# Attention's last turns in a fused attention, expert and dense kernel: choice of two groups behind the scores, first expert slot a turn earlier, v weighted three chunks ahead

## The chip, the cores and the metric

The kernel runs on one core of a Trainium2 chip. The metric is the device time of one execution in microseconds; lower is better.

## What is computed

A decayed linear attention over 4 x 768 tokens with 8 heads of 64, then a choice of one of 8 experts for each of the 3072 tokens with that expert's two-layer network, then a dense two-layer network. Cut from the reference:

```python
def _attn_ref(q, k, v):
    gamma = 1.0 - 2.0 ** (-5.0 - np.arange(H))
    for t in range(S):
        state = gamma * state + einsum('bhd,bhe->bhde', k[:, :, t], v[:, :, t])
        y[:, :, t] = scale * einsum('bhd,bhde->bhe', q[:, :, t], state)

def _moe_ref(x, modality_id, w_gate, modality_bias, w1, w2):
    logits = x @ w_gate + modality_bias[modality_id]
    e_idx = np.argmax(logits, axis=1)
    gate_w = softmax(logits)[arange(N), e_idx]
    for e in range(E):
        h = np.maximum(x[mask] @ w1[e], 0.0)
        out[mask] = gate_w[mask, None] * (h @ w2[e])

def _moe2_ref(x, w_in, w_out):
    h = x @ w_in
    return (h * sigmoid(1.702 * h)) @ w_out
```

## The kernel before

The work has three stages. **Attention** goes through NT = 24 chunks of 128 tokens in the loop `for n in range(LAST + 1)` (L861). One pass of this loop is called turn n here. The order of the instructions in the source is the order on each engine: the schedule is written by hand, and every engine (PE for matrix products, DVE and ACT for copies and element work, POOL for gathers and scatters, SP for loads) works through its own list in order.

In turn n a chunk passes through these helpers. `emit_prep` (L217) multiplies v by the decay on POOL and gives vs; before, it runs for chunk n + 2, with three buffers. `emit_scores` (L225) makes the scores pss of chunk n + 1 on PE (L231) and their masked copies A on DVE (L235, two of them). `emit_state` (L251) adds to the running state pst (L262) and copies it on ACT (ssb, L265). `emit_av` (L268) makes the chunk's output psy on PE (L279, L282), `emit_rows_k` (L238) turns the next keys (pkn L244, copy kn L246), `emit_xt` (L286) scales the output on DVE (xT, L290). One turn later `emit_rows` (L293) turns it into rows (pxr L297, copy xr L299) and writes them to memory (xd, from ACT's queue, L300), and `emit_gate` (L302) makes the gate's products (pm L305, copy lt on ACT L307). Two turns later `emit_logits` (L310) makes the logits (pl L311 on PE, lg L312 on DVE).

Tokens are sorted by expert in groups of GS = 3 chunks. `emit_group` (L314) is the choice: DVE works from the logits to ohall (L318 to L327), ACT makes ex (L321). `emit_rank` (L330) is the rank of each token within its expert: small products on PE (L334 to L339), then DVE arithmetic (L341 to L350) into posi and idg. `emit_scatter` (L352) writes them to the table `order` in memory by three indirect transfers from POOL (L354). Before, the choice of a group stands at the end of the turn that made its last logits, and its ranks in the next turn, after the state.

The **expert stage** works in slots of 256 tokens of one expert (`run_slots`, L633). `places` reads a slot's piece of `order` into ix (POOL, L641), `gather` fetches its rows xg (POOL, L650), `prep` turns them (pxt on PE L673, xh on ACT L676, xl on DVE L677). A slot has eight units: four of `b1` (first layer, 24 products L689 each, then hh on ACT L694 and hl on DVE L695) and four of `second` (second layer, 24 products pso, L707), in the order b1 0, b1 1, second 0, b1 2 and so on. Weights come as 512 KB loads raw from SP (L572, four buffers) and are split in two by `split` (L574): whi, a cast on ACT (L593), and wlo, a subtraction on DVE (L595). After each unit two more weights are split.

The first EARLY = 18 chunks' tokens suffice for two slots, whose table (`table_early`, L390) follows the ranks of chunks 15 to 17. Before, that is in turn 20; the slot's generator is then advanced by one step a turn (`next(slots)`), except in turn NT - 1 = 23. The first three steps only issue places and gathers; the fourth, in turn 24, turns the rows and does the first b1. EARLY_SPLIT splits one weight in turn 22 and two in turn 23, ahead of the slot. The loop ends with turn LAST = 26. The other slots follow after the final table (`table_final`, L410), which needs the last group's ranks.

The **dense stage** (`d1` L1094, `d2` L1114) runs from about 440 us to the end.

## Time and profile before

| | us |
|---|---|
| median of three runs | 999.86 |
| lowest and highest | 993.59, 1003.96 |
| profiled execution | 1001.46 |
| its span, first to last instruction | 999.8 |
| PE busy | 965.2 |
| DVE, ACT, POOL busy | 503.1, 410.7, 179.1 |

The span is what the trace shows; the profiled execution's time has 1.7 us around it. Times in the trace count from the span's start. In the timelines a bracket gives the idle time of the engine just before a row and what ended it. Attention takes about the first 134 us, the expert stage runs to about 440.

In the trace a turn can be told by its gate products (L305), which are those of chunk n - 1: turn 20 ends with them at 112.2, turn 21 at 118.4, turn 22 at 128.0, turn 23 at 132.3 and turn 24's at 134.3.

### The profile page before, as it was taken

Reading aid. Unit: us, or ns where it says so; the run is one execution under the profiler, and the core shown is the slowest. Engines: PE = TensorE matmul, PEld = TensorE weight load, DVE = VectorE, ACT = ScalarE, POOL = GpSimd, SP = SyncE. Lnnn points to the kernel's source line nnn. Section 1 sums busy time; section 2 is a strip of 40 time slices with the busy share of each in tenths; the row PEclk is TensorE's granted clock in tenths of the full one; section 3 lists DMA queues with packets and bytes.
Section 4 is the critical chain, followed back from the end, with each engine's and each line's share of the span. In section 5 each row is a group of like instructions: output and inputs, shape, how many; then the busy total and the mean of one; then the engine's idle time right before and its main releaser. Section 6 shows DMA issues by size and latency. Waiting matters only on the chain.

```text
span 999.8 us, 16732 instructions
## 1 busy us (share of the span) xinstructions
PE 965.2 (97%) x6610; PEld 855.2 (86%) x6610; DVE 503.1 (50%) x921; ACT 410.7 (41%) x728; POOL 179.1 (18%) x177
## 2 busy tenths in 40 slices
PE   8999879999999999999999999999999999999995
PEld 7888668899999987879999999998999998999994
DVE  3555568798888876449942322323323223223221
ACT  3433245576777665348732222222322223222221
POOL 2343334233322222003310010010100100100101
PEclk9999999999999999999999999999999999999998
DMA  8787689888888879925310100100001001000000
GB/s 288 225 217 199 126 217 227 265 271 285 284 266 270 282 242 333 324 67 177 127 43 1 33 32 1 33 32 22 27 17 32 32 1 33 32 1 1 32 1 31
DMA packets 43128, 128.18 MB, mean 128 GB/s; under 512 B 6976, under 2 KB 7360, under 8 KB 43040
## 3 DMA queue, kind: packets, MB, share of 16 engines
q1 hardware_dynamic: 34464, 107.96, 35.0%
q0 software_dynamic: 5120, 12.77, 3.7%
q10 hardware_dynamic: 3456, 6.29, 1.9%
q8 instruction: 53, 0.87, 0.4%
q14 instruction: 35, 0.29, 0.1%
HBM read 107.76 MB, written 19.24 MB: 127 GB/s over the span
## 4 chain that ended last, share of the span: by engine, by line
PE 54%; ACT 0%; DVE 0%; POOLq 0%; POOL 0%; issue 0%; ACTq 0%
PE psq L1121 27%; PE psd L1100 26%; PE pyt L1027 1%; ACT L1103 0%; POOLq L1187 0%; DVE ab L961 0%; DVE ab L963 0%; ACT o L1127 0%; ACT ab L956 0%; ACT ab L966 0%; ACT sig L1103 0%; DVE gl L1111 0%; DVE ab L962 0%; POOL out_dram L1129 0%; POOLq L1129 0%
## 5 line engine op out<-in xcount | busy, mean ns | idle before, releaser
L1105 DVE TENSOR_TENSOR g<-psd,sig 128x384 f32<-128x384 f32 x128 | 71.3, 557 | 279.7 <-ACT sig L1103 279.7
L1103 ACT ACTIVATE sig<-psd 128x384 f32<-128x384 f32 x128 | 62.9, 492 | 289.5 <-PE psd L1100 289.5
L1100 PE MATMUL psd<-yl,wih 128*128 128x384 f32 x512 | 172.1, 336 | 0.0
L1100 PE MATMUL psd<-yh,wil 128*128 128x384 f32 x512 | 171.9, 336 | 0.0
L1100 PE MATMUL psd<-yh,wih 128*128 128x384 f32 x512 | 171.6, 335 | 0.2 <-PEq L1076 0.2
L1121 PE MATMUL psq<-woh,gh 128*128 128x512 f32 x384 | 153.9, 401 | 0.7 <-ACT gh L1110 0.7
L1121 PE MATMUL psq<-woh,gl 128*128 128x512 f32 x384 | 152.2, 396 | 1.1 <-DVE gl L1111 1.1
L1121 PE MATMUL psq<-wol,gh 128*128 128x512 f32 x384 | 152.3, 397 | 0.0
L595 DVE TENSOR_TENSOR wlo<-raw,whi 128x1024 fp32r<-128x1024 f32 x93 | 113.4, 1224 | 32.6 <-ACT whi L593 29.3
L593 ACT CAST whi<-raw 128x1024 fp32r<-128x1024 f32 x96 | 99.9, 1046 | 42.0 <-issue 16.6
L689 PE MATMUL psh<-xh,whi 128*128 128x256 f32 x384 | 109.5, 285 | 0.2 <-ACT xh L676 0.2
L689 PE MATMUL psh<-xl,whi 128*128 128x256 f32 x384 | 107.9, 281 | 0.3 <-DVE xl L677 0.3
L689 PE MATMUL psh<-xh,wlo 128*128 128x256 f32 x384 | 107.7, 281 | 0.0
L1129 POOL DMA_INDIRECT out_dram<-o,idd x24 | 23.3, 973 | 462.5 <-DVE o L1125 387.5
L1111 DVE TENSOR_TENSOR gl<-g,gh 128x384 fp32r<-128x384 f32 x128 | 71.7, 560 | 65.0 <-ACT gh L1110 65.0
L1100 PEld LDWEIGHTS psd<-yh,wih 128*128 128x128 f32 x512 | 96.5, 188 | 6.3 <-PEq L1076 0.6
L1100 PEld LDWEIGHTS psd<-yl,wih 128*128 128x128 f32 x512 | 96.0, 188 | 5.8
L1100 PEld LDWEIGHTS psd<-yh,wil 128*128 128x128 f32 x512 | 96.1, 188 | 0.0
L1110 ACT CAST gh<-g 128x384 fp32r<-128x384 f32 x128 | 65.8, 514 | 70.3 <-DVE g L1105 70.2
L1121 PEld LDWEIGHTS psq<-woh,gl 128*128 128x128 f32 x384 | 72.1, 188 | 19.0 <-DVE gl L1111 1.5
L1121 PEld LDWEIGHTS psq<-woh,gh 128*128 128x128 f32 x384 | 72.0, 188 | 13.0 <-ACT gh L1110 1.0
L1121 PEld LDWEIGHTS psq<-wol,gh 128*128 128x128 f32 x384 | 72.3, 188 | 11.6
(195 smaller groups left out, 1516.4 us busy)
## 6 DMA issues: line engine op xcount, KB each, us to landing
raw<-in_w_dram SPq DMA_DIRECT2D x96, 512.0 KB
qk<-in_qn_dram SPq DMA_DIRECT2D x23, 512.0 KB
r<-in_w_in_dram SPq DMA_DIRECT2D x16, 512.0 KB
r<-in_w_out_dram SPq DMA_DIRECT2D x16, 512.0 KB
ys<-yo SPq DMA_DIRECT2D x12, 513.0 KB
yg<-ys SPq DMA_DIRECT2D x24, 256.5 KB
v<-in_kv_dram SPq DMA_DIRECT2D x24, 256.0 KB
xd<-xr ACTq DMA_DIRECT2D x24, 256.0 KB
```

The lines of the kernel that those rows point to most:

```text
L593: nc.scalar.copy(hi, raw)
L595: eng.tensor_tensor(out=lo, in0=raw, in1=hi.bitcast(F32), op=ALU.subtract)
L689: nc.tensor.matmul(ps[:, f, :], a[:, k, f * C:(f + 1) * C], b[:, k, :], start=(m == 0), stop=(m == 11), skip_group_check=True)
L1027: nc.tensor.transpose(ps[:, k, :], y[:, k * C:(k + 1) * C], ident)
L1100: nc.tensor.matmul(ps, a[:, k, f * C:(f + 1) * C], b[:, k, :], start=(m == 0), stop=(m == 11), skip_group_check=True)
L1103: nc.scalar.activation(sig, ps, AF.Sigmoid, scale=1.702)
L1105: V.tensor_tensor(out=g, in0=ps, in1=sig, op=ALU.mult)
L1110: nc.scalar.copy(gh, g)
L1111: V.tensor_tensor(out=gl, in0=g, in1=gh.bitcast(F32), op=ALU.subtract)
L1121: nc.tensor.matmul(PO[t][r], a[:, r * C:(r + 1) * C], b[f], start=(f == 0 and m == 0), stop=(f == NF - 1 and m == 2), skip_group_check=True)
L1129: nc.gpsimd.indirect_dma_start(out=outv[n], out_offset=bass.IndirectOffsetOnAxis(ap=idd[:, n:n + 1], axis=0), in_=o, in_offset=None)
```

## The change

Three things are moved.

- `emit_prep` runs for chunk n + 3 in turn n, with four buffers of vs, and three times ahead of the loop.
- For the two groups that end with chunks 17 and 20 (SOON), the turn in which their last logits are due makes the logits and the choice right behind the scores, ahead of the state, and the ranks and the scatter in the same turn. The first slot's table and generator therefore begin in turn 19, and the first b1 stands in turn 23. EARLY_SPLIT is set a turn earlier.
- At the end, the logits of chunk 23 follow its gate in turn 24, with the choice, and the last ranks come in turn 25, which is now the last. The scatter is issued ahead of the slot's step.

```diff
--- before.py
+++ after.py
@@ -218,7 +218,7 @@
         c = n % NC_
         d = st[n] = {}
         v = loads[n][3]
-        vs = wp.tile([C, H, D], F32, name="vs", tag="vs", bufs=3)
+        vs = wp.tile([C, H, D], F32, name="vs", tag="vs", bufs=4)
         nc.gpsimd.tensor_tensor(out=vs, in0=v, in1=b3(o1(M("kc")[:, 8 * c:8 * c + 8]), H, D), op=ALU.mult)
         d.update(vs=vs)
 
@@ -531,7 +531,7 @@
         return out_
 
     POOL = lambda i, kind: i in (9, 11, 13) or kind == 'S' and i % 2
-    EARLY_SPLIT = {NT - 2: 1, NT - 1: 2}
+    EARLY_SPLIT = {NT - 3: 1, NT - 2: 2}
 
     class Stream:
 
@@ -857,7 +857,9 @@
     load(3)
     grp = rank = slots = None
     mps = ExitStack()
-    LAST = NT + 2
+    emit_prep(2)
+    LAST = NT + 1
+    SOON = (EARLY - 1, EARLY + GS - 1)
     for n in range(LAST + 1):
         if n + AHEAD < NT:
             load(n + AHEAD)
@@ -866,18 +868,22 @@
         if n == 0:
             emit_state(0)
             emit_av(0)
-        if n + 2 < NT:
-            emit_prep(n + 2)
+        if n + 3 < NT:
+            emit_prep(n + 3)
         if n + 1 < NT:
             emit_scores(n + 1)
         if n + 1 < NC_:
             decay(n + 1)
-        if 0 < n < NT:
-            emit_state(n)
         m = n - 2
         pl = None
         if m >= 0:
             pl = ps_1.tile([C, 512], F32, name="pl", tag="pl")
+        soon = m in SOON
+        if soon:
+            emit_logits(m, grp, m % GS, pl)
+            emit_group(m - GS + 1, grp)
+        if 0 < n < NT:
+            emit_state(n)
         if n == 1:
             setup()
         scat = None
@@ -890,38 +896,44 @@
             emit_rows_k(n + 1)
         if n < NT:
             emit_xt(n)
+        if soon:
+            emit_rank(m - GS + 1, grp, pl)
+            scat = m - GS + 1
         if n == NT - 1:
             psl.close()
             open_psum(mps)
         if 0 <= n - 1 < NT:
             emit_rows(n - 1)
-        if 0 <= m < NT:
+        if 0 <= m < NT - 1 and not soon:
             if m % GS == 0:
                 grp = {"l": gp.tile([C, GS, E], F32, name="lg", tag="lg")}
             emit_logits(m, grp, m % GS, pl)
         if 0 <= n - 1 < NT:
             emit_gate(n - 1, ps_1.tile([C, C], F32, name="pm", tag="pm"))
+        if n == NT:
+            emit_logits(NT - 1, grp, GS - 1, pl)
+            m = NT - 1
+        if 0 <= m < NT and m % GS == GS - 1 and not soon and n <= NT:
+            emit_group(m - GS + 1, grp)
+            rank = (m - GS + 1, grp)
         if rank and n == LAST:
             emit_rank(*rank, pl)
             scat, rank = rank[0], None
-        if 0 <= m < NT and m % GS == GS - 1:
-            emit_group(m - GS + 1, grp)
-            rank = (m - GS + 1, grp)
-        if slots is not None:
-            if n != NT - 1:
-                next(slots)
-            if n < NT:
-                SS.split(EARLY_SPLIT.get(n, 0))
         if scat is not None:
             if scat + GS == EARLY:
                 for _ in table_early():
                     pass
             emit_scatter(scat)
-            if scat + GS == EARLY:
-                SS.limit, SS.ns = 8 * NP1, NP1
-                slots = run_slots(SS)
+        if slots is not None:
+            if n != NT - 2:
                 next(slots)
-                SS.load()
+            if n < NT:
+                SS.split(EARLY_SPLIT.get(n, 0))
+        if scat is not None and scat + GS == EARLY:
+            SS.limit, SS.ns = 8 * NP1, NP1
+            slots = run_slots(SS)
+            next(slots)
+            SS.load()
     psr.close()
     pa.close()
     open_more(mps)
```

The masks of the scores of chunk 23 (A) and the choice of chunks 18 to 20 on DVE, from xT of chunk 21 on, before:

```order
L290 TENSOR_TENSOR xT<-psy,qc 128x512
L312 TENSOR_TENSOR lg<-pl,brow 128x8
L235 TENSOR_TENSOR A<-pss,misc 128x512 x2
L290 TENSOR_TENSOR xT<-psy,qc 128x512
L312 TENSOR_TENSOR lg<-pl,brow 128x8
L318 TENSOR_REDUCE mx<-lg 128x3
L319 TENSOR_TENSOR lg<-lg,mx 128x24
L324 SCALAR_TENSOR_TENSOR cand<-lg,misc 128x24
L326 TENSOR_REDUCE best<-cand 128x3
L327 TENSOR_TENSOR ohall<-best,misc 128x24
L595 TENSOR_TENSOR wlo<-raw,whi 128x1024
```

and on the same engine at the same place after the change:

```order
L290 TENSOR_TENSOR xT<-psy,qc 128x512
L312 TENSOR_TENSOR lg<-pl,brow 128x8
L595 TENSOR_TENSOR wlo<-raw,whi 128x1024
L235 TENSOR_TENSOR A<-pss,misc 128x512 x2
L312 TENSOR_TENSOR lg<-pl,brow 128x8
L318 TENSOR_REDUCE mx<-lg 128x3
L319 TENSOR_TENSOR lg<-lg,mx 128x24
L324 SCALAR_TENSOR_TENSOR cand<-lg,misc 128x24
L326 TENSOR_REDUCE best<-cand 128x3
L327 TENSOR_TENSOR ohall<-best,misc 128x24
L290 TENSOR_TENSOR xT<-psy,qc 128x512
```

The first weight's subtraction wlo has moved ahead of the masks and the choice, and xT of chunk 22 behind it.

The rows of chunk 23 (xr, lt) and the first slot's casts on ACT, before:

```order
L299 COPY xr<-pxr 128x512
L300 DMA xd<-xr 128x512
L307 COPY lt<-pm 128x128
L676 CAST xh<-pxt 128x512 x2
L694 ACTIVATE hh<-psh 128x512
L593 CAST whi<-raw 128x1024 x2
L321 ACTIVATE ex<-lg 128x24
```

and on ACT after the change:

```order
L676 CAST xh<-pxt 128x512 x2
L694 ACTIVATE hh<-psh 128x512
L593 CAST whi<-raw 128x1024 x2
L299 COPY xr<-pxr 128x512
L300 DMA xd<-xr 128x512
L307 COPY lt<-pm 128x128
L321 ACTIVATE ex<-lg 128x24
```

The copies xr and lt have moved behind the first b1's hh and the two casts.

The end of the first b1 (L689) and the beginning of the second on PE, before:

```order
L689 MATMUL psh<-xh,wlo 128x256
L311 MATMUL pl<-misc,lt 128x8
L689 MATMUL psh<-xh,whi 128x256
L689 MATMUL psh<-xl,whi 128x256
L689 MATMUL psh<-xh,wlo 128x256
```

and on PE after the change:

```order
L689 MATMUL psh<-xh,wlo 128x256
L297 MATMUL pxr<-misc,xT 128x128 x4
L311 MATMUL pl<-misc,lt 128x8
L305 MATMUL pm<-xT,wgs 32x128 x4
L311 MATMUL pl<-misc,lt 128x8
L689 MATMUL psh<-xh,whi 128x256
```

The rows and the gate of chunk 23 and both last logits (the first L311 is chunk 22's, the second chunk 23's) now stand between the two units; before, chunk 23's rows and gate and chunk 22's logits stood ahead of the first.

## Rows read from the trace of the kernel before

**Rows 1.** The page's part 1: busy time of each engine, share of the span, instructions.
```profile
PE 965.2 (97%) x6610; PEld 855.2 (86%) x6610; DVE 503.1 (50%) x921; ACT 410.7 (41%) x728; POOL 179.1 (18%) x177
```

**Rows 2.** Windows: stretch, length, busy us by engine (instructions), PE clock, DMA share, GB/s.
```profile
115.00:120.00 5.00, 3.08 (x41) 2.43 (x40) 1.98 (x3) 0.37 (x1) 0.00 (x0) 1.00 1.26 51
120.00:125.00 5.00, 2.97 (x48) 2.64 (x48) 1.46 (x3) 1.71 (x4) 2.19 (x3) 0.82 0.63 185
125.00:130.00 5.00, 4.02 (x64) 3.22 (x58) 1.84 (x8) 1.91 (x4) 1.03 (x1) 0.84 0.74 290
145.00:150.00 5.00, 4.23 (x18) 3.40 (x18) 4.32 (x12) 2.69 (x4) 0.00 (x0) 0.70 0.88 200
200.00:240.00 40.00, 40.00 (x266) 36.62 (x265) 36.35 (x56) 28.39 (x39) 13.30 (x10) 1.00 0.81 277
```

**Rows 3.** PE's timeline: start, us, engine, line, operation, count, idle before and releaser.
```profile
107.09 1.16 PE L231 MATMUL pss<-qk 64*128 64x128 f32 x16
...
112.16 1.16 PE L231 MATMUL pss<-qk 64*128 64x128 f32 x16
...
122.03 1.16 PE L231 MATMUL pss<-qk 64*128 64x128 f32 x16 [3.63 <-ACT kn L246]
...
129.00 0.17 PE L334 MATMUL pl<-ohall,tri 128*128 128x24 bf16 x1 [0.98 <-DVE ohall L327]
...
133.17 0.63 PE L297 MATMUL pxr<-misc,xT 128*128 128x128 f32 x4 [0.86 <-DVE lg L312]
...
135.70 0.98 PE L673 MATMUL pxt<-misc,xg 128*128 128x128 f32 x7 [1.16 <-DMA xg<-xd,ix]
...
137.65 0.38 PE L689 MATMUL psh<-xl,whi 128*128 128x256 f32 x1 [0.34 <-DVE xl L677]
...
145.77 0.17 PE L334 MATMUL pl<-ohall,tri 128*128 128x24 bf16 x1 [2.12 <-DVE ohall L327]
```

**Rows 4.** ACT's timeline at the end of attention.
```profile
121.39 0.59 ACT L246 COPY kn<-pkn 128x512 f32<-128x512 f32 x1 [5.40 <-remote]
...
131.54 0.59 ACT L299 COPY xr<-pxr 128x512 f32<-128x512 f32 x1 [1.65 <-PE pxr L297]
...
132.53 0.27 ACT L307 COPY lt<-pm 128x128 f32<-128x128 f32 x1 [0.40 <-PE pm L305]
...
140.63 0.60 ACT L694 ACTIVATE hh<-psh 128x512 fp32r<-128x512 f32 x1 [3.28 <-PE psh L689]
141.13 1.99 ACT L593 CAST whi<-raw 128x1024 fp32r<-128x1024 f32 x2
```

**Rows 5.** DVE's timeline at the end of attention.
```profile
106.84 0.17 DVE L312 TENSOR_TENSOR lg<-pl,brow 128x8 f32<-128x8 f32 x1 [0.44 <-PE pl L311]
...
107.90 0.18 DVE L327 TENSOR_TENSOR ohall<-best,misc 128x24 bf16<-128x24 f32 x1
...
111.99 0.16 DVE L365 TENSOR_TENSOR t_cnt<-base,misc 128x8 f32<-128x8 f32 x1
...
123.22 1.29 DVE L235 TENSOR_TENSOR A<-pss,misc 128x512 f32<-128x512 f32 x2 [1.48 <-PE pss L231]
...
133.77 2.36 DVE L595 TENSOR_TENSOR wlo<-raw,whi 128x1024 fp32r<-128x1024 f32 x2 [0.68 <-ACT whi L593]
```

**Rows 6.** POOL's timeline at the end of attention.
```profile
108.22 1.04 POOL L222 TENSOR_TENSOR vs<-v,misc 128x512 f32<-128x512 f32 x1 [5.57 <-DMA v<-in_kv_dram]
111.14 1.00 POOL L354 DMA_INDIRECT order<-idg,posi  x1 [1.88 <-DVE idg L350]
...
122.20 0.59 POOL L641 DMA_DIRECT2D ix<-order  x1 [7.50 <-DVE lg L312]
...
128.82 1.03 POOL L650 DMA_INDIRECT xg<-xd,ix  x1 [4.41 <-DMA ix<-order]
```

**Rows 7.** SP's queue: the first four weight loads.
```profile
114.63 2.02 SPq L572 DMA_DIRECT2D raw<-in_w_dram  x4
```

**Rows 8.** PE's timeline where slot 2's rows are turned.
```profile
181.32 0.33 PE L673 MATMUL pxt<-misc,xg 128*128 128x128 f32 x1 [1.65 <-DMA xg<-xd,ix]
```

## The prediction

> **What bounds the kernel now.** I read the page's busy line first [rows 1]: TensorE (PE) is busy for 965.2 of 999.8 us, so an edit can only pay where PE idles or runs at a lower clock. The windows come next [rows 2]: the expert stage has PE full (40.00 of 40 us at clock 1.00 in 200:240), and the hole lies where attention ends, from 115 on: 115:120 has PE busy 3.08 of 5 us, 120:125 2.97 of 5 at a granted clock of 0.82, 125:130 0.84, and 145:150 0.70: TensorE spent parts of these at 1.2 instead of 2.4 GHz, after stretches in which it had idled. Last I read PE's own timeline there [rows 3], whose brackets name each wait. Adding them up: 3.63 (scores wait for the copy of kn), 0.98 (ranks wait for the choice), 0.86, 1.16 (transposes wait for gathered rows), 0.34, 2.12 (the last ranks wait for the last choice). Clock: (0.18 + 0.16) x 5 = 1.7 us lost in 120:130 and 0.30 x 5 = 1.5 us in 145:150.
>
> A turn of attention is 5.07 us of nearly unbroken PE work (107.09 to 112.16 [rows 3]). So starting the first slot a turn earlier moves no PE work away; it only changes which waits lie between the pieces. The forecast is a balance of waits.
>
> **What goes.** The ranks of chunks 18 to 20 and the last ranks now follow their choice in another way: the last choice is issued before the second b1 instead of behind it, so its 2.12 us go. The first b1 stands ahead of the last chunk's rows, so the waits in the old places (0.98, 0.86, 1.16, 0.34) go too, as far as new ones don't replace them. Together 5.46 us.
>
> **What comes at the early choice (turn 19).** The logits stand behind the scores; the choice is a DVE chain of 1.24 us (lg at 106.84 to the end of ohall at 108.08 [rows 5]) behind the two masks A (1.29). It ends some 2.6 us after the scores, while PE has about 3 us of state, values and row transposes to do before the ranks: no wait. The ranks' numbers are then ready near 108.1. The scatter doesn't start then: on POOL it is queued behind vs of chunk 22, which in the trace ran at 108.22 because v had only then arrived (5.57 us wait [rows 6]) and takes 1.05. So the scatter starts at about 109.3 instead of 111.14, 1.8 us sooner; vs three chunks ahead needs v a turn earlier and that costs POOL a wait, not PE. The table on DVE started at 111.99 [rows 5] and the weights' first load went at 114.63 [rows 7], 2.64 later; with the table at 108.1 the weights go at about 110.8, 3.8 us sooner.
>
> **The stall behind the first weight loads.** From 114.63 to 122.03 nearly everything halts: 115:120 moves 51 GB/s with the DMA engines busy 1.26 of the time, POOL waits 7.50 us for the scatter to land [rows 6], ACT's copy of kn starts at 121.39 after 5.40 us [rows 4], and PE idles. I can't name the cause; it begins where the first four 512 KB loads are issued, so I let it move with them, 7.4 us long. It then runs from 110.8 to 118.2. PE finishes turn 20 near 113.1 (turn 19 now carries logits and ranks, and 5.07 us follow) and idles 5.1 us. Before it was 3.63, and 0.3 more inside 115:120 (1.9 us idle there, of which 1.6 are the 3.63's beginning): 4.0. Cost +1.1; bounds +1.5 (PE a little earlier still) and -5.7 (no stall: the 4.0 us and the clock's 1.7).
>
> **New wait 1, ranks of turn 22.** Count from the end of turn 21's gate matmuls. ACT copies lt by +0.8, then casts whi (about 1.0) to +1.75. The first wlo now stands on DVE ahead of chunk 23's masks: 1.2 to +2.95, masks to +4.2, chain to +5.5. PE has 3.6 us of work before the ranks, so it waits 1.9 and ends the turn at +6.6. ACT's and DVE's durations are those of [rows 4, 5].
>
> **New wait 2, start of the first b1.** ACT: lt to +7.5, two casts to +9.4. DVE: two wlo (2.36) to +10.8, xT 0.69, lg, xl 0.7, to +12.3. PE's own work (values, rows, gate, 2.75, and the transposes 1.15) ends at +10.5: it waits 1.8 where 0.34 stood. The gathered rows: in the trace 24.6 us lie between the scatter's start (111.14) and the transposes (135.70). From 109.3 that gives 133.9; PE comes with stall and half-clock stretch at 118.2 + 4.9 + 1.7 + 9.35 = 134.2, so the gather is just hidden; bound +1.5 if it is later.
>
> **New wait 3, the last logits.** Behind the first b1 PE does rows, logits of 22 and the gate of 23 (1.1 us), then the logits of 23, in order ahead of the second b1. These need lt of 23, and ACT has hh (0.6) and two casts (1.99 at 141.13 [rows 4]) queued ahead of xr and lt; xr to the end of lt is 1.3 us (131.54 to 132.80 [rows 4]). That is 3.9 us after the b1's end, and DVE reads the logits of 22 only behind hl and two wlo, about the same. PE waits 3.9 + 0.2 - 1.1 = 3.0 us. In the old order lt was copied ahead of xh, and no wait stood there. Bounds 2.0 (casts overlapping more) and 3.3.
>
> **Sum.** 1.9 + 1.8 + 3.0 - 5.46 = +1.2; with the stall +1.1, +2.3 us. The clock: one low stretch behind the stall, one behind the 3.0 us wait, in place of two: 0 (bounds -1.5, +1.7). The profiled execution took 1001.46 us and would become 1003.8. It lies 1.6 above the median of 999.86, inside the spread of the runs (993.59 to 1003.96); against the median the forecast is 1002.2. Behind the second b1 the orders are alike, and PE is full, so a shift there reaches the end.
>
> **A rule weighed.** POOL waited 7.50 us for the scatter to land and the gather 4.41 more for ix, 128.82 being 14.2 us after the first weight load [rows 6, 7]. The Trainium skill, "DMA: Bandwidth & Descriptors", section on queues, rings and completion order, says that a transfer's semaphore write lands only after every earlier write of that DMA engine, in whatever queue. The two waits agree with it; no run here shows it alone. By that rule small transfers end no sooner than the weights begun before them, and the weights now begin before two of the three scatters.
>
> **Rivals.**
> 1. The forecast, chance 0.5: 1002.2.
> 2. The stall is not tied to the weights and doesn't come, chance 0.2. For: the loads of the expert stage show none (277 GB/s in 200:240 [rows 2]). Against: it begins within about a microsecond of the first loads. Sum +1.2 - 5.7 = -4.5: 995.4. As a mechanism of this kernel, if ix still came 14.2 us after the first weight load (125.0) and the rows 6.9 us later (128.82 to 135.70), at 131.9, PE would reach the transposes at 113.1 + 4.9 + 9.35 = 127.3 and the first b1 would start at 134.3 instead of 130.3, 4.0 late: 999.4. By the rule above this second number holds.
> 3. The change does what it says: DVE and ACT get ahead of PE because it is the one held up, new waits 1 and 2 vanish (-3.7), and the second low stretch of the clock with them (-1.5): 997.0. Chance 0.15. Against: ACT's and DVE's queues are in order and the casts are ahead.
> 4. Slower: the gather of slot 2. In the trace PE waited 1.65 us for it at 181.32 [rows 8]. The last scatter waits for the ranks' numbers, which DVE now computes behind hl and two wlo, with PE not waiting there any more. If that chain is not paced by PE, the wait grows by the 2.12 us that PE no longer loses at the last ranks, and a third low stretch of the clock adds 1.7: 1006.0. It decides once the last scatter starts later behind the last ranks than hl, two wlo (2.36) and the 1.3 us of rank arithmetic explain. Chance 0.15.
>
> **How the numbers follow.** A measurement of this kernel tells about 1% (10 us) from no change; the runs of before alone spread that far. All four cases lie within it. Faster by over 1% needs case 2 and 3 at once: 0.07. Slower by over 1% needs 4 and a longer stall: 0.05. The range runs from rival 2 less the clock's 1.5 (993.9) to rival 4 plus 1.
>
> **What would show it.** Right: scatter of the first groups near 109.3, weights issued near 111, a PE stop of about 5 us right behind turn 20; a wait of 1 to 2 us at the ranks of turn 22; a wait of about 3 us at the second L311 behind the first b1, ended by ACT lt or DVE lg; no wait at the last ranks. Wrong: no stop after the first loads, or the last logits passing without a wait.

## The result, and the profile after the change

The changed kernel is slower: a median of 1009.58 us (1005.84 to 1013.30, six runs) against 998.27 us (993.59 to 1003.96, six runs) for the kernel before, ratio 1.0106 with a 95% interval of 1.0076 to 1.0137. The forecast was 1002.2 us with a range up to 1007.0: wrong by 7.4 us, and outside its range. The profiled execution took 1005.84 us, the fastest of the six, so its span of 1004.2 (before 999.8) shows 4.4 us of a loss whose median is 11.3. More than that was lost behind turn 19, though: its gate products start at 102.90 here and at 106.73 in before, 3.8 us sooner with no less work done. That lead isn't the change's doing as far as the traces tell, since the same code has them anywhere up to 112.56 (last section); from turn 19 to the end this execution lost 4.4 + 3.8 = 8.2 us.

The page's busy line, as [rows 1]: PE's work is the same, 0.2 us apart.

```profile
PE 965.4 (96%) x6610; PEld 856.9 (85%) x6610; DVE 507.3 (51%) x921; ACT 410.6 (41%) x728; POOL 177.6 (18%) x177
```

The windows of the same stretches, as [rows 2], and 160:200 besides (stretch, length, busy us by engine with instructions, granted clock of PE, DMA share, GB/s):

```profile
115.00:120.00 5.00, 3.52 (x66) 2.99 (x65) 3.04 (x7) 1.58 (x5) 0.00 (x0) 1.00 1.21 268
120.00:125.00 5.00, 4.23 (x51) 3.13 (x51) 4.73 (x13) 3.02 (x6) 2.19 (x3) 0.66 0.75 279
125.00:130.00 5.00, 1.05 (x14) 0.76 (x14) 1.54 (x3) 0.85 (x2) 3.56 (x4) 0.84 0.72 225
130.00:135.00 5.00, 2.42 (x9) 1.83 (x9) 0.38 (x1) 0.73 (x2) 1.58 (x2) 0.50 0.38 144
135.00:140.00 5.00, 4.85 (x28) 4.64 (x28) 1.00 (x2) 0.60 (x2) 1.95 (x2) 0.64 0.54 105
...
145.00:150.00 5.00, 5.00 (x32) 4.69 (x31) 1.24 (x4) 1.58 (x3) 0.00 (x0) 0.66 0.54 204
160.00:200.00 40.00, 34.45 (x210) 30.64 (x209) 31.15 (x81) 16.37 (x21) 13.35 (x11) 0.96 0.72 213
```

The hole has moved and grown: 125:135 has PE busy 3.47 of 10 us (before 7.60), and the granted clock is below 1 in six of the seven stretches shown. Adding (1 - clock) x 5 over 120 to 150 gives 8.5 us where [rows 2] and the rest of before's windows give 3.2; part of that lies in time in which PE idles anyway.

PE's own timeline, as [rows 3] and [rows 8], with each wait in its bracket:

```profile
120.46 0.17 PE L334 MATMUL pl<-ohall,tri 128*128 128x24 bf16 x1 [1.94 <-DVE ohall L327]
...
131.52 0.48 PE L673 MATMUL pxt<-misc,xg 128*128 128x128 f32 x1 [5.47 <-DMA xg<-xd,ix]
133.06 1.76 PE L673 MATMUL pxt<-misc,xg 128*128 128x128 f32 x7 [1.06 <-DMA xg<-xd,ix]
...
143.99 0.36 PE L311 MATMUL pl<-misc,lt 128*128 128x8 f32 x2 [3.27 <-DVE lg L312]
...
148.41 0.24 PE L334 MATMUL pl<-ohall,tri 128*128 128x24 bf16 x1
...
167.50 0.50 PE L707 MATMUL pso<-whi,hl 128*128 128x512 f32 x1 [3.30 <-DVE hl L695]
...
186.54 0.69 PE L673 MATMUL pxt<-misc,xg 128*128 128x128 f32 x2 [2.00 <-DMA xg<-xd,ix]
```

Read them in order. The ranks of turn 22 wait 1.94 us: forecast 1.9. The transposes of the first slot wait 5.47 + 1.06 us for the gathered rows: forecast "just hidden". The last logits wait 3.27 us: forecast 3.0. The last ranks have no bracket: forecast none. Then a wait that the forecast doesn't have, 3.30 us for hl in the middle of a second layer; before it was 0.27.

These waits come to 15.04 us (1.94, 5.47, 1.06, 3.27, 3.30) where before has 9.36 (the six of [rows 3] and 0.27). Of the 8.2 us some 2.5 are left (an estimate) for the lower clock and the smaller gaps.

The 3.27 us are two queues that end together, as the forecast had them. ACT has hh, two casts, xr and lt in a row; lt ends at 143.75. DVE has hl, two wlo and then lg of chunk 22, which ends at 143.84 and is what PE's bracket names; PE starts 0.15 us behind it.

```profile
139.84 0.60 ACT L694 ACTIVATE hh<-psh 128x512 fp32r<-128x512 f32 x1 [4.40 <-PE psh L689]
140.33 1.98 ACT L593 CAST whi<-raw 128x1024 fp32r<-128x1024 f32 x2
142.21 0.59 ACT L299 COPY xr<-pxr 128x512 f32<-128x512 f32 x1
...
143.48 0.27 ACT L307 COPY lt<-pm 128x128 f32<-128x128 f32 x1 [0.68 <-ACT xr L299]
```

```profile
141.40 2.36 DVE L595 TENSOR_TENSOR wlo<-raw,whi 128x1024 fp32r<-128x1024 f32 x2 [0.24 <-ACT whi L593]
143.68 0.16 DVE L312 TENSOR_TENSOR lg<-pl,brow 128x8 f32<-128x8 f32 x1
```

POOL and SP, as [rows 6] and [rows 7]. The three scatters begin 7 us sooner than before, the weights 8.3 us sooner, and these now go out before the third scatter. POOL then waits 13.54 us for the scatters (before 7.50), with vs of chunk 23 queued behind:

```profile
104.16 1.00 POOL L354 DMA_INDIRECT order<-idg,posi  x1 [4.40 <-DVE sm L348]
105.47 0.97 POOL L354 DMA_INDIRECT order<-idg,posi  x1 [0.30 <-issue]
106.75 0.97 POOL L354 DMA_INDIRECT order<-idg,posi  x1 [0.30 <-DVE rB L365]
121.25 0.59 POOL L641 DMA_DIRECT2D ix<-order  x1 [13.54 <-PE pxr L297]
121.86 1.06 POOL L222 TENSOR_TENSOR vs<-v,misc 128x512 f32<-128x512 f32 x1
...
125.53 1.23 POOL L650 DMA_INDIRECT xg<-xd,ix  x1 [2.06 <-DMA ix<-order]
```

```profile
106.37 1.94 SPq L572 DMA_DIRECT2D raw<-in_w_dram  x4
```

The bracket names PE's pxr because that ended last by the records; PE's pxr has nothing to do with ix, and the same wait is put down to the transfer of order in four of the experiments below.

The wait for hl, on DVE and on POOL:

```profile
157.85 3.04 DVE L367 SCALAR_TENSOR_TENSOR t_mB<-t_nbig,t_n 128x8 f32<-128x8 f32 x1
...
163.53 2.42 DVE L365 TENSOR_TENSOR t_sc<-t_cB,misc 128x104 f32<-128x104 f32 x1
...
166.77 0.68 DVE L695 SCALAR_TENSOR_TENSOR hl<-psh,hh 128x512 fp32r<-128x512 f32 x1
```

```profile
158.44 2.41 POOL L595 TENSOR_TENSOR wlo<-raw,whi 128x1024 fp32r<-128x1024 f32 x1
162.67 3.17 POOL L595 TENSOR_TENSOR wlo<-raw,whi 128x1024 fp32r<-128x1024 f32 x1 [1.82 <-ACT whi L593]
```

Two operations of the final table (`table_final`), of 8 and 104 elements a partition, take 3.04 and 2.42 us where their neighbours take 0.16 to 0.27. They end at 160.89 and 165.95; POOL's two subtractions end at 160.85 and 165.84. The hl that PE waits for stands behind the second one. Before has the same sight once, on DVE and POOL, the two ending 0.11 us apart:

```profile
155.07 2.72 DVE L365 TENSOR_TENSOR t_sc<-t_n,misc 128x96 f32<-128x96 f32 x1
```

```profile
155.28 2.40 POOL L595 TENSOR_TENSOR wlo<-raw,whi 128x1024 fp32r<-128x1024 f32 x1
```

By milestones: the first product of the second layer starts at 148.63 (before 145.92, +2.7), slot 2's second layer 6 us later than before, the dense stage's first product 2.8 later, the end of the span 4.4.

### The profile page after: what moved, and what is told of

The parts are those of the page before. It is cut to its first block, busy times and chain, and to the rows that moved or that the text cites. A ratio compares the mean times of both kernels' runs of the same rounds, so it can differ in the third digit from the quotient of the medians.

```text
span 1004.2 us, 16734 instructions
## 1 busy us (share of the span) xinstructions
PE 965.4 (96%) x6610; PEld 856.9 (85%) x6610; DVE 507.3 (51%) x921; ACT 410.6 (41%) x728; POOL 177.6 (18%) x177
## 4 chain that ended last, share of the span: by engine, by line
PE 54%; ACT 0%; DVE 0%; POOLq 0%; POOL 0%; issue 0%; ACTq 0%
PE psq L1133 27%; PE psd L1112 26%; PE pyt L1039 1%; ACT L1115 0%; POOLq L1199 0%; DVE ab L973 0%; DVE ab L975 0%; ACT o L1139 0%; ACT ab L968 0%; ACT ab L978 0%; ACT sig L1115 0%; DVE gl L1123 0%; DVE ab L974 0%; POOL out_dram L1141 0%; POOLq L1141 0%
## 5 line engine op out<-in xcount | busy, mean ns | idle before, releaser
L689 PE MATMUL psh<-xh,whi 128*128 128x256 f32 x384 | 110.6, 288 | 0.0
L689 PE MATMUL psh<-xl,whi 128*128 128x256 f32 x384 | 109.1, 284 | 0.1
L689 PE MATMUL psh<-xh,wlo 128*128 128x256 f32 x384 | 109.1, 284 | 0.0
```

What stands on the lines that cost most here:

```text
L689: nc.tensor.matmul(ps[:, f, :], a[:, k, f * C:(f + 1) * C], b[:, k, :], start=(m == 0), stop=(m == 11), skip_group_check=True)
```

## The experiments

Three suspects: the early weight loads (they go out amid the scatters), the order around the first b1 (it stands ahead of the last logits), and wlo on POOL (it meets the final table on DVE); and v three chunks ahead as a fourth. Each ratio is against runs of the kernel before on the same chip. Brackets hold 95% intervals.

### Each suspect alone

**Weight loads later, in the changed kernel (e1) and in the one before (e2).** The expert numbers that SP reads for the loads are copied a turn later, so the loads start later too; the rest stays.

```diff
-        V.tensor_copy(eB[:, 0:NP1], e_)
...
         if slots is not None:
+            if n == EARLY + 2:
+                V.tensor_copy(eB[:, 0:NP1], T("eb", MAXB)[:, 0:NP1])
...
-            SS.load()
```

(e2: the same in the kernel before, with EARLY + 3.)

> The changed kernel with one edit: the expert numbers of the first slots are written one turn later (the copy of eB moves from the table in turn 19 to the end of turn 20), so the first weight loads go near 110 instead of 106.4 us, after all three scatters. Theory A (the scatter's landing, which ix waits for, is held up by weight loads issued in its midst): POOL's wait ahead of the first ix falls from 13.5 us to under 4, the first transposes wait under 1 us in place of 5.5 and 1.1, the low stretch of the clock there (0.50 in 130:135) goes; 8 to 11 us faster than the changed kernel, about 999. Theory B (the long landing comes from the scatter itself or from attention's own transfers): the wait before ix stays above 10 us, the time stays within 2 us of the changed kernel.

Measured: ratio 1.0005 [0.9979, 1.0031], 1.0% less than the changed kernel's. The loads go out 2.47 us behind the third scatter's start instead of 0.38 ahead of it, POOL's wait falls from 13.54 to 6.77 (I had expected under 4), and PE has no wait for the rows of the first slot. The waits for the last logits (3.27) and for hl (3.45) stay, and that at the ranks of turn 22 grows to 4.54, since the first cast now waits 2.50 us for its weights on ACT, and on DVE the wlo stands behind it and the choice behind the wlo. POOL's row of e1:

```profile
115.78 0.59 POOL L640 DMA_DIRECT2D ix<-order  x1 [6.77 <-DMA order<-idg,posi]
```

> The kernel before with the same edit: eB is written a turn later (end of turn 21), so the first weights go near 119 instead of 114.6 us. Theory A: POOL's 7.5 us wait before ix falls to under 3, and the halt of 115 to 122 (ACT's copy of kn 5.4 us late, PE's wait of 3.6) goes; 3 to 6 us faster than before, about 994. Theory B: the halt stays where it was, the time is that of before.

Measured: 0.9988 [0.9959, 1.0018], no difference that shows. In before the loads already start 0.90 us behind the third scatter, and POOL's wait is 7.02 us here against 7.50. So this cure is one for the changed kernel.

**The first b1 behind the last logits (e3).**

```diff
-            if n != NT - 2:
+            if n not in (NT - 2, NT - 1):
+                next(slots)
+            if n == NT:
                 next(slots)
```

> The changed kernel with the first b1 moved from turn 23 to turn 24, behind the last logits and choice, both first units in that turn. Theory A: the wait of 3.3 us at the last logits falls to about 1.2 (lt no longer behind hh and two casts) and the low clock stretch behind it goes, while the wait for the gathered rows shrinks by the 2.5 us of work that now stands ahead of it: 4 to 7 us faster than the changed kernel, about 1004. Theory C (the gathered rows alone set the time, the logits' wait is hidden by something later): no more than 2 us faster.

Measured: 1.0037 [1.0004, 1.0070], 0.7% less than the changed kernel. The wait at the last logits falls from 3.27 to 0.53. POOL still waits 12.91 us for the scatters, PE 2.02 for vs of chunk 23 (queued behind that wait), 1.86 for the rows, 3.55 for hl.

**v three chunks ahead, alone, in the kernel before (e4).**

```diff
-        vs = wp.tile([C, H, D], F32, name="vs", tag="vs", bufs=3)
+        vs = wp.tile([C, H, D], F32, name="vs", tag="vs", bufs=4)
...
+    emit_prep(2)
...
-        if n + 2 < NT:
-            emit_prep(n + 2)
+        if n + 3 < NT:
+            emit_prep(n + 3)
```

> The kernel before with only v weighted three chunks ahead. Theory A: it is what made attention's turns earlier in the changed kernel (turn 19's gate at 102.9 in place of 106.7 us), by taking vs out of PE's way: turns 14 to 20 come 3 to 4 us earlier, and the whole is 2 to 4 us faster, about 995. Theory D (those turns' difference is chance in the transfers): turns within 1 us of before or scattered, time within 1 us of before.

Measured: 1.0026 [0.9998, 1.0054]: no gain. In this execution the loads went out 0.37 us behind the third scatter's start, and POOL waited 12.43 us: the kernel before can fall into the long wait as well. Turn 19's gate products start at 101.08 instead of 106.73, but as v three ahead has them up to 112.56 in other kernels, that isn't shown to be the edit's doing.

**The early splits a turn later (e6).**

```diff
-    EARLY_SPLIT = {NT - 3: 1, NT - 2: 2}
+    EARLY_SPLIT = {NT - 2: 3}
```

> The changed kernel with the three early splits all in turn 22, instead of one in turn 21 and two in turn 22. If the wait at the ranks of turn 22 (1.94 us) is made by the first wlo on DVE ahead of chunk 23's masks, as the forecast has it, it falls by about 1.2 to 0.5 to 0.9 us; rival: it is made by ACT's copies and stays at 1.6 us or more. Theory A: PE then only comes sooner to the gathered rows, whose time the scatters and the weights set, so the 5.5 us wait at pxt grows by what the ranks lose and the time stays at the changed kernel's, ratio to before 1.006 to 1.013. Rival: the gather is paced by PE through the scatters; then the time falls by 1 to 2 us more, ratio 1.003 to 1.008.

Measured: 1.0101 [1.0015, 1.0188]. The wait at the ranks of turn 22 is gone (none over 0.3 us), so it was made by the wlo ahead of chunk 23's masks. The time is the changed kernel's: PE waits 3.97 us for vs of chunk 23, whose multiplication stands on POOL behind the scatters' wait, and 4.64 + 2.06 for the rows.

**wlo off POOL (e7).**

```diff
-    POOL = lambda i, kind: i in (9, 11, 13) or kind == 'S' and i % 2
+    POOL = lambda i, kind: kind == 'S' and i % 2
```

> The changed kernel with the wlo subtractions 9, 11 and 13 on DVE instead of POOL. Theory C (a subtraction of 128x1024 on POOL holds up small table operations on DVE that run beside it: 3.04 and 2.42 us where the like takes 0.16 to 0.26): no t_ operation on DVE between 140 and 175 us takes over 0.6 us, and the wait for hl at the first pso of second 2 (3.30 us) falls under 1.5 us although DVE has three more subtractions of 1.2 us. The time falls by 1 to 4 us against the changed kernel, ratio to before 1.006 to 1.011. Rival: the long table operations are long by themselves (their operands come late from elsewhere): they stay over 2 us, the wait for hl grows to 4 us or more, ratio 1.010 or more.

Measured: 1.0011 [0.9976, 1.0047], 0.95% less than the changed kernel. The same two operations on DVE, in e7:

```profile
164.64 0.16 DVE L367 SCALAR_TENSOR_TENSOR t_mB<-t_nbig,t_n 128x8 f32<-128x8 f32 x1
...
167.45 0.26 DVE L365 TENSOR_TENSOR t_sc<-t_cB,misc 128x104 f32<-128x104 f32 x1
```

0.16 and 0.26 instead of 3.04 and 2.42, no wait for hl over 0.3 us though DVE has three subtractions more, and the clock in 160:200 is 1.00 instead of 0.96. The wait for the rows is there as before (5.88 us), so this cause is a second, separate one. The gain in time (9.5 us between the ratios) was larger than I had expected (1 to 4 us) and than the wait that went; what else it consists of isn't shown. The edit also takes a subtraction out of POOL's queue ahead of slot 2's ix (see e10), and PE's wait there falls from 2.00 to 1.33 us.

### How the weights hold the scatters

**Two turns later (e8), and only two loads at first (e9).**

```diff
+            if n == EARLY + 3:
+                V.tensor_copy(eB[:, 0:NP1], T("eb", MAXB)[:, 0:NP1])
...
-            if n < NT:
+            if EARLY + 2 < n < NT:
                 SS.split(EARLY_SPLIT.get(n, 0))
```

(e8; with the deletions of e1 and the early splits of e6.)

> The changed kernel with the first weight loads held back two turns, to the end of turn 21, and the three early splits in turn 22. Theory A: the scatters are alone, so POOL waits 3 us or less for them at L641 (13.54 in the changed kernel, 6.77 with the loads held back one turn); the gather xg is issued within 4 us of ix and PE waits under 0.5 us at the first pxt. The weights come later: the first casts whi wait for raw, and PE waits 1 to 4 us at the first b1 for whi or wlo. Ratio to before 0.994 to 1.002. Rival: the scatter's landing has nothing to do with the weights (loads of q, k and v in flight hold it, or its own descriptors): POOL's wait stays at 6 us or more, and the ratio is 1.002 or more, since the weights now come late too.

Measured: 1.0016 [0.9977, 1.0054]. With the loads 9.55 us behind, the scatters still hold POOL for 5.97 us, twice what I had expected: that much comes without any weight load. POOL then waits only 0.95 us for ix. But now the loads, from 119.42 on, stand beside the gather of the rows, and PE waits there:

```profile
127.68 0.33 PE L672 MATMUL pxt<-misc,xg 128*128 128x128 f32 x1 [2.78 <-DMA xg<-xd,ix]
...
133.01 1.33 PE L672 MATMUL pxt<-misc,xg 128*128 128x128 f32 x5 [5.00 <-DMA xg<-xd,ix]
```

The second gather was issued at 121.30 and its rows came 11.7 us later. As it looks, the 2 MB are to be kept clear of each of the three small transfers in the chain (scatter, ix, xg); for ix and xg no run tests that alone.

```diff
-            SS.limit, SS.ns = 8 * NP1, NP1
+            SS.limit, SS.ns = 2, NP1
...
+            if n == EARLY + 3:
+                V.tensor_copy(eB2, T("eb", MAXB)[:, 0:NP1])
+                SS.limit = 8 * NP1
```

(e9; from the third load on SP reads the expert's number from eB2.)

> The changed kernel, but only two of the first four 512 KB weight loads go right behind the scatters; the other two go at the end of turn 21. Theory A, by amount (a scatter's landing waits until the weights begun before it are through): alone it waited 5.97 us (weights two turns later), with four loads 13.54, so with two 8.5 to 11 us at L641; the gathered rows then meet the other two loads, and PE's wait at pxt stays at 3 us or more; time as the changed kernel or 1 to 5 us less. Rival 1 (any load in flight holds it, whatever the amount): 12.5 us or more. Rival 2 (only the third and fourth load fall behind the scatter): under 7.5 us.

Measured: 1.0116 [1.0063, 1.0169]; POOL waits 14.81 us, as rival 1 of that expectation has it. But this doesn't rule out the amount: the other loads went out from 120.24 on, when POOL had waited 7.5 us and had 7.3 more to wait.

```profile
120.24 0.86 SPq L575 DMA_DIRECT2D raw<-in_w_dram  x2
```

More is seen when all kernels are set side by side, by how long after the third scatter's start the first load was issued:

```
kernel   third scatter  first load   behind by   POOL waits at ix
e3           108.79        107.88       -0.91         12.91
after        106.75        106.37       -0.38         13.54
e6           108.91        108.53       -0.38         13.37
e7           111.99        111.61       -0.38         13.72
e9           111.76        111.39       -0.37         14.81
e13          111.26        110.89       -0.37         12.97
e4           108.92        109.29       +0.37         12.43
before       113.73        114.63       +0.90          7.50
e10          114.83        115.78       +0.95          7.50
e1           108.05        110.52       +2.47          6.77
e5           109.67        112.14       +2.47          7.29
e14          112.40        115.78       +3.38          6.28
e12          115.66        119.25       +3.59          6.93
e11          116.42        120.02       +3.60          6.51
e2           109.93        113.89       +3.96          7.02
e15          113.51        120.05       +6.54          5.92
e8           109.87        119.42       +9.55          5.97
```

A step, not a slope: up to +0.37 us 12.4 to 14.8, from +0.90 on 5.9 to 7.5. The step lies inside the 0.97 us that POOL takes to issue a scatter. That one edit moves a kernel across it is shown twice, by e1 (13.54 to 6.77) and e13 below (6.51 to 12.97). The Trainium skill, "DMA: Bandwidth & Descriptors", section "Queues, rings and completion order", has the rule that fits: a completion is written only after all earlier writes of that DMA engine, whatever queue they came from. The step agrees with it; no run shows the rule alone.

While a scatter is under way the loads themselves crawl. The DMA queue rows (packets, MB, share of 16 engines' time) of the changed kernel in 107:113, amid the scatters, and of e8 in 119:122, long after them:

```profile
q1 hardware_dynamic: 86, 0.35, 108.8%
```

```profile
q1 hardware_dynamic: 112, 0.46, 51.4%
```

1.088 x 16 x 6 us / 86 = 1.21 us for a packet of 4 KB, against 0.514 x 16 x 3 / 112 = 0.22. That is the stall behind the first loads that the forecast spoke of; why a few hundred entries of 8 bytes do this, no run here shows. It is not what doubles POOL's wait: in e1 the loads crawl as well (37 packets and 67.1% in 108.5:115, 1.9 us each).

### Together, and one left out

**First attempt (e5)**: e1, e3 and e6 in one kernel.

> The changed kernel with three edits: first weight loads held back to the end of turn 20, the first b1 behind the last logits, and all three early splits in turn 22. Theory A (weight loads issued amid the scatters hold up the scatters' landing, so the gather ends late): POOL waits at most 7 us for ix's release at L641, and PE waits under 1 us at pxt of the first slot. Theory B (the wait of 3.27 us at the last logits comes from hh and two casts queued ahead of lt on ACT): it falls under 0.6 us. Forecast's own new wait 1 (the first wlo stands ahead of chunk 23's masks on DVE): the wait at the ranks of turn 22 falls from 1.94 to under 0.9 us. If all three hold: PE's whole idle time falls from 26.9 to about 20 us and the ratio to before is 0.992 (0.987 to 0.998). Rival: ACT and DVE have the same work left in the same stretch, so the waits only move to the first b1 (hl, whi) and to the last ranks; then the idle time stays over 23 us and the ratio is 0.999 or more.

Measured: 1.0016 [0.9976, 1.0057]. The wait at the last logits (0.53) and at the ranks are as expected, POOL's wait 7.29. But the three splits of turn 22 free three buffers, so three more loads go out between 124.69 and 127.30, amid the issue of the two gathers (123.95 and 125.86), and PE waits 8.15 us for the rows; 3.63 for hl. Waits moved, as the rival said.

**wlo off POOL in the kernel before (e10)**, with the edit of e7.

> The kernel before with the wlo subtractions 9, 11 and 13 on DVE instead of POOL. Theory C says that the collision of small DVE operations with a POOL subtraction is there in before too (t_sc 2.72 us in 155:158) but that before has the slack: its wait for hl is 0.27 us. No t_ operation over 0.9 us then, no wait over 0.6 us that hl ends, and the time as before: ratio 0.996 to 1.002. Rival (the three subtractions on POOL pay for themselves in before): DVE is late instead, a wait of 1 us or more for wlo or hl between 150 and 185 us, ratio 1.002 or more. Third: in other executions of before the collision falls as badly as after the change, then the ratio is 0.995 or less.

Measured: 0.9961 [0.9933, 0.9988]. So before pays for wlo on POOL too. Its stretched t_sc (2.72 us) delays not hl but the final table. What is gone in e10 are the waits for slot 2's rows, 1.65 [rows 8] and, behind it, 0.36 us: PE has no wait over 0.3 us between 148 and 200. The collision is not the main reason for that, as the rows read. DVE had rB, which ix needs, ready at 166.62 in before, but on POOL the third subtraction stood ahead of ix, and ix went out 3.7 us later; in e10 it is 1.2 us behind rB (167.26). POOL of before, then of e10:

```profile
168.01 2.41 POOL L595 TENSOR_TENSOR wlo<-raw,whi 128x1024 fp32r<-128x1024 f32 x1 [4.09 <-ACT whi L593]
170.35 1.17 POOL L641 DMA_DIRECT2D ix<-order  x2
```

```profile
168.50 0.58 POOL L641 DMA_DIRECT2D ix<-order  x1 [11.59 <-DVE yo L714]
```

So the edit removes two things, the collision and a place in POOL's queue, and no run parts them in time; that the wait for hl is the collision's is seen on DVE, where the stretched operations stand ahead of hl.

**Both cures in the changed kernel (e12)**: e1 and e7.

> The changed kernel with the first weight loads at the end of turn 20 and wlo 9, 11 and 13 on DVE. Theories A and C are of different places (110 to 130 and 150 to 170 us), so what each alone gave, about 1% against the changed kernel, adds up: ratio to before 0.992 (0.988 to 0.998); the wait at the last logits stays at 3.27 us, that for hl is under 1 us. Rival: whatever PE comes sooner with is lost to the gather of the third slot (waits at pxt near 185 us of 4 us or more) or at the final table: ratio 0.999 or more.

Measured: 0.9969 [0.9940, 0.9997]. The two gains of about 1% don't add up: 1.4% together.

**All three (e11)**: e1, e3, e7, and the early splits at {NT - 2: 1, NT - 1: 2}, as before the change, so that fewer loads stand ahead of the gather.

> The changed kernel with four edits: first weight loads at the end of turn 20, the early splits in turns 22 and 23 (one and two), the first b1 in turn 24 behind the last logits, and wlo 9, 11 and 13 on DVE. Theories A, B and C together: POOL waits at most 7.5 us at L641, PE waits under 1 us each at the ranks of turn 22, at the last logits and for hl, and under 2 us at the first pxt, since no further weight load stands ahead of the gather. PE's whole idle time 14 to 20 us (before 22.7), ratio to before 0.990 (0.985 to 0.997). Rival: with three splits on ACT and DVE right ahead of the first b1, the first b1 waits 3 us or more for whi or wlo; ratio 0.998 or more.

Measured: 0.9938 [0.9909, 0.9967], median 995.67 against 1001.69: faster than before, and by the ratios than the changed kernel. PE's windows where the hole was:

```profile
120.00:125.00 5.00, 5.00 (x90) 4.25 (x88) 2.15 (x4) 1.88 (x5) 1.09 (x2) 1.00 0.91 123
125.00:130.00 5.00, 5.00 (x99) 3.91 (x99) 4.08 (x17) 1.51 (x6) 1.09 (x2) 1.00 1.01 390
130.00:135.00 5.00, 2.77 (x40) 2.05 (x36) 3.33 (x5) 4.08 (x6) 3.88 (x4) 0.97 0.69 198
135.00:140.00 5.00, 3.20 (x12) 2.42 (x13) 2.83 (x10) 1.66 (x4) 2.06 (x3) 0.50 0.91 284
```

No wait at the ranks of turn 22, 0.51 us for the rows, 0.55 for hl. The last logits still wait 2.18 us, for DVE, where I had expected under 1.

**e11 with the weights early again (e13)**: only the deletions and the copy of e1 undone.

> The kernel of e11 with only the first weight loads back right behind the slot's start, as in the changed kernel. Theory A in its sharper form (the wait at L641 steps up when the first weight load is issued before POOL has issued the third scatter): the load is issued less than 0.5 us behind the third scatter's start or ahead of it, POOL waits 12 to 15 us at L641 (6.51 in e11), vs of chunk 23 is late behind it (PE waits 1 to 4 us at L282), and PE waits 2 to 6 us at pxt. Ratio to before 0.997 to 1.003, so 0.4 to 0.9% over e11. Rival: with the first b1 in turn 24 there is time enough for the scatter's wait; PE's waits stay under 1 us and the ratio is that of e11, 0.991 to 0.996.

Measured: 0.9961 [0.9936, 0.9986]. The long wait is back (12.97 us), and PE waits 2.51 for vs of chunk 23 and 1.38 + 0.55 for the rows:

```profile
126.92 1.09 PE L282 MATMUL psy<-A,vs 128*64 128x128 f32 x16 [2.51 <-POOL vs L222]
...
135.39 0.47 PE L673 MATMUL pxt<-misc,xg 128*128 128x128 f32 x1 [1.38 <-DMA xg<-xd,ix]
```

In time it is 0.2% above e11, with intervals that overlap, so no price shows: with the first b1 a turn later, most of the scatters' wait is hidden. The mechanism is as expected.

**e11 with wlo on POOL again (e14)**: only the edit of e7 undone.

> The kernel of e11 with only wlo 9, 11 and 13 back on POOL. Theory C: at least one t_ operation on DVE takes over 2 us and ends within 0.2 us of a POOL wlo's end, and where it stands ahead of an hl, PE waits 3 us or more for hl; the wait for pxt of the third slot grows from 1.09. Ratio to before 0.997 to 1.002, 0.3 to 0.8% over e11. Rival: the collision falls where DVE has slack, as in before; no wait for hl over 1 us, ratio 0.991 to 0.996.

Measured: 0.9982 [0.9959, 1.0006], 0.4% above e11, with intervals that just overlap. The collision and the wait for hl return, here on DVE, POOL and PE of e14:

```profile
152.57 2.88 DVE L367 SCALAR_TENSOR_TENSOR t_mB<-t_nbig,t_n 128x8 f32<-128x8 f32 x1
...
156.97 3.27 DVE L594 TENSOR_TENSOR wlo<-raw,whi 128x1024 fp32r<-128x1024 f32 x1
```

```profile
153.00 2.42 POOL L594 TENSOR_TENSOR wlo<-raw,whi 128x1024 fp32r<-128x1024 f32 x1
156.79 2.37 POOL L594 TENSOR_TENSOR wlo<-raw,whi 128x1024 fp32r<-128x1024 f32 x1 [1.38 <-ACT whi L592]
```

```profile
161.97 0.50 PE L706 MATMUL pso<-whi,hl 128*128 128x512 f32 x1 [3.63 <-DVE hl L694]
```

t_mB ends at 155.45, wlo at 155.42. The second victim is not a small operation this time but DVE's own subtraction: 3.27 us instead of 1.2, ending 1.08 us behind POOL's second.

**The kernel before with the two cures (e15)**: e2 and e10, none of the change's moves.

> The kernel before with the first weight loads at the end of turn 21 and wlo 9, 11 and 13 on DVE. If the change's own moves gain nothing (its waits replace those it removes, as the forecast's sum has it), this is as fast as e11: ratio to before 0.992 to 0.997. If the moves gain what they remove (0.98, 1.16 and 2.12 us of waits at the ranks and the transposes, some 0.3 to 0.4%), this stays at 0.996 to 1.000 and e11 is the faster by 0.3% or more.

Measured: 0.9942 [0.9916, 0.9968], as fast as e11. Its PE waits where the change wanted to save:

```profile
124.65 0.17 PE L334 MATMUL pl<-ohall,tri 128*128 128x24 bf16 x1 [0.98 <-DVE ohall L327]
...
134.97 1.76 PE L672 MATMUL pxt<-misc,xg 128*128 128x128 f32 x7 [2.57 <-DMA xg<-xd,ix]
...
146.27 0.17 PE L334 MATMUL pl<-ohall,tri 128*128 128x24 bf16 x1 [2.15 <-DVE ohall L327]
```

It keeps the 0.98 and 2.15 us that the change removes, and e11 without them is no faster: e11 waits 2.18 us at the last logits instead, and 1.19 at the chunk's row transposes (0.86 in e15). Over the whole span PE isn't busy for 32.6 us in e15 (995.1 less 962.5) and 31.4 in e11 (996.5 less 965.1). e11 has the first b1 and the early splits back where before has them, so this speaks of the moves that it keeps: v, the early choice and the last logits and ranks.

## Why the prediction was wrong

**Right.** That PE's work doesn't change and the balance is one of waits. New wait 1 (1.9 forecast, 1.94 measured, and its cause shown by e6). New wait 3 (3.0 forecast, 3.27 measured; e3, which takes the b1 and with it both queues from ahead of it, brings it to 0.53). The last ranks without a wait. That the moves gain nothing by themselves: e15 against e11, for those that e11 keeps.

**The step that failed: "the gather is just hidden".** The forecast carried the 24.6 us from the scatters' start to the transposes over from before, and set PE's arrival 24.9 us behind that start. Both were off, in the bad direction. (That the scatters began at 104.16 and not near 109.3 is for the most part the 3.8 us by which this execution was ahead.) The chain took 28.9 us (104.16 to 133.06), because the first load went out before the third scatter and POOL waited 13.54 us instead of 7.50. The forecast itself had put the weights "before two of the three scatters" and quoted the rule for what follows, and then left it out of the sum: a transfer moved past another needs its duration worked out anew, not the old one shifted. The forecast's own times (scatters from 109.3 on, 1.3 us apart, loads at 110.8) put the first load ahead of the third scatter; the bound of +1.5 was 5 too small.

**The other half of that step: "I let it move with them".** The forecast moved the stall behind the first loads as a stop of PE of 5.1 us right behind turn 20. PE had no wait over 0.4 us from 100 to 118: "no stop after the first loads", the forecast's own sign of being wrong. What stalls are the transfers (59 GB/s in 107:113, the DMA engines' share above 1). In before PE's stop came by way of the copy of kn, which stood still for 5.40 us with a releaser that the trace calls only "remote" [rows 4]; in the changed kernel ACT had a like wait of 3.34 us ahead of one copy (ssb, 107.59), and PE hardly felt it. What these two copies waited for isn't known. So PE reached the transposes 21.9 us after the scatters' start (126.06), three sooner than assumed, and paid 6.5 us there in one piece. New wait 2 (1.8) vanished in it: the first b1 starts without a wait behind the transposes. Rival 2 had PE's side of this, no stop and an arrival 18.0 us behind the scatters' start (127.3 less 109.3), but it too carried a time over from before: 14.2 us from the first load to the gather, which took 19.2 (106.37 to 125.53). Its first b1 at 134.3 isn't worked out from the rows' 131.9; it decides nothing here.

**The term that was missing: hl.** Nothing in the forecast speaks of the final table meeting POOL's wlo. It could have been read in before: t_sc with 2.72 us (shown above) among neighbours of 0.16 to 0.26. The change moved the table and the wlo against each other so that the stretched operations came ahead of an hl that PE waits for: 3.30 us, and a clock of 0.96 in 160:200 where before had 1.00. e7 shows the cause by removing it, e14 by putting it back, for the wait; how much of e7's gain in time is this wait, no run shows.

**The clock: forecast 0.** More and longer waits gave more low stretches, 8.5 us by the sum above against 3.2; how much of the difference is loss and how much lies in idle time, the windows don't separate. The balance above leaves some 2.5 us for it and the small gaps together.

Rival 4 named slot 2's gather: it waits 2.25 us in all instead of 2.01 (1.65 [rows 8] and 0.36), not 2.12 more, so that rival's mechanism didn't come, though the time came out on its side. What stays open: the profile accounts for 8.2 us from turn 19 on, the medians for 11.3. The executions without a profile show no waits, so where the rest of the median goes isn't known; and the gains of e1, e3 and e7 (1.0, 0.7, 0.95%) overlap rather than add.

## What to carry to other kernels

A chain of small dependent transfers (scatter, index, gather) is best kept clear of bulk loads (shown here for the scatters): issue the bulk behind the last small transfer, not amid them, and re-time the chain whenever one is moved past the other. Before a change that shifts two engines against each other, look in the old trace for single operations that take ten times what their neighbours take: they show what the new alignment can hit. And a saved wait in a hand-written order is worth nothing until the next wait on the same queue is known: here the two cures in the old order gave 0.6% (e15), and what e11 keeps of the reordering nothing on top.

## What the hardware showed that I had not expected

**DVE waits for POOL, wholly.** In all eleven kernels with wlo 9, 11 and 13 on POOL, one or two operations of the final table (8 to 104 elements a partition, with two tiles as operands but for a t_cB in e2 and e4) took 2.1 to 3.05 us, each ending within 0.15 us of the end of a POOL subtraction; in the six with wlo on DVE those operations took no longer than their neighbours. In all seventeen kernels one more, t_off near 200 us with 8 elements, took 1.25 to 1.27 us instead of 0.16, ending within 0.04 us of another POOL operation (sg, 2.14 us in e10). Which ones are hit, and whether an hl stands behind them, differs with the alignment. A DVE subtraction at 162.40 in the changed kernel kept its 1.21 us, and POOL's beside it took 3.17 instead of 2.41. The Trainium skill, "SBUF — State Buffer", section "Who interferes with whom", says that DVE and GpSimd share a port pair as an exclusive lock, and that whoever comes second waits for the other's whole instruction. The trace agrees for t_sc, which starts within POOL's subtraction and ends with it (163.53 in 162.67 to 165.84), and for that POOL subtraction, which starts 0.27 us behind DVE's. It doesn't tell for t_mB, whose record begins 0.59 us ahead of POOL's (157.85, 158.44) and which waits all the same. The price is 9 to 19 times the small operation's own time.

**A scatter of 3 x 128 entries of 8 bytes holds its successor for 6 us without a weight load beside it** (5.97 in e8, 5.92 in e15), and packets of a load beside it take 1.21 us instead of 0.22.

**Attention itself comes at different times.** The third scatter starts at 109.93, 113.51, 113.73 and 114.83 in four kernels that are alike up to there (e2, e15, before, e10), a spread of 4.9 us, half of 1% of the span. In the twelve kernels that have the change's code up to there, the gate products of turn 19 start between 102.90 (the changed kernel) and 112.56 (e11), 9.7 us apart. A forecast of a few us for what follows can't be held against single profiles.
